# Logits' table on all partitions, T's copies ahead of V's last part, and four smaller moves in the front of a fused FFT, soft-MoE and ReLU² kernel

## The chip, the core and the metric

The kernel runs on one core of a Trainium2 chip. The metric is device time in microseconds: the median of several executions, before and after the change. The core has TensorE (matrix products into PSUM), VectorE, ScalarE and GpSimd for the rest, SyncE, whose queue issues nearly all transfers, and 16 DMA engines. In the rows PE is the matmuls of TensorE and PEld its weight loads; DVE is VectorE, ACT ScalarE, POOL GpSimd, SPq the queue of SyncE.

## The reference

The input x is 8 x 3072 x 256 in float32. Three layers follow one another:

```python
X = fft(fft(x, axis=1), axis=2).real                  # 24576 x 256
logits = X @ phi                                      # 8 experts x 4 slots
d = exp(logits - max over the 3072 positions); d /= d.sum(0) + 1e-9
c = exp(logits - max over the 32 slots);       c /= c.sum(1) + 1e-9
slots = d.T @ X;  slots = relu(slots @ w1[e]) @ w2[e] # per expert
Y = c @ slots                                         # 24576 x 256
out = (s * relu(Y @ w_in)**2 + b) @ w_out             # w_in 256 x 2048, w_out 2048 x 256, in float64
```

In the code the reshape to tokens runs over the batch and the positions of the FFT, and the maximum over a column is taken over all rows of the eight sequences together.

## The kernel before, in words

**Stages.** The FFT is never formed for logits: phi is folded into the DFT along the model dimension, and the DFT along the positions is split into 128 and 24. The front has five stages. (1) x comes in 24 pages of 1 MB, three for each of the eight sequences b. `emit_v(n)` (n = 2b and 2b + 1; the last is n = 15) multiplies pages by the folded phi (L394), copies the sum to `vts` (L406); `turn_v` transposes it (L415) and copies it to `v` (L419); `emit_t(b)` applies the DFT over 128 (L450, or L428 and L439 for the last b) and copies to `tt` (L464; L462 for b = 6; L432 and L445 for b = 7). (2) Logits: nine steps of products of `tt` with `ltab`, the table of the DFT over 24 (L570), for two halves of the partitions, h = 0 and 1; each sum is copied to `lg` (L583) and reduced to a column maximum (L585). The maxima are reduced again (L589, L592), transposed (L598), reduced (L603) and spread to all partitions as `cmb` (L608). (3) `lg - cmb` (L633, alternately VectorE and GpSimd), exp (L669), products with `htab`, the table of the second direction (L652). (4) The r stage: DFT of that and its sum with x's pages in another layout, `xrt` (24 pages of 1 MB, L326; products at L727). (5) The experts (w1, w2, 16 MB). Then the main loop over 64 blocks of 384 tokens, with the products at L1121, L1151 and L1154.

**Pages.** x, raw weights, tables and `xrt` share a ring of 15 pages of 8 KB per partition (20 from logits on). `page` takes one and `drop` gives it back; a transfer into a page waits for the last reader of the page's tile before. A string, `ORDER`, gives the order in which SyncE's queue gets its transfers in the front: x a page of x, w a quarter of w_out, r a page of `xrt`, l a page of `ltab`, h a page of `htab`. Eight transfers can be outstanding on that queue: the trace shows each issue behind the landing of the eighth before it.

**w_out** comes in float64 in four quarters, k = 0 to 3. A quarter is a list of side steps that the front hands out one at a time: five passes of VectorE that make float32 of it (s1 to s5), a maximum (L222), its sum into the bias on GpSimd (L276), its scale (L204, L205), the part rounded to f16 on ScalarE (`cast`, L212), and two steps `low`, the rest that rounding leaves (L216). For the last quarter, six steps (with two of the third quarter) stand before `emit_v(15)`, five in the rest of stage 1 and the two of `low` behind the logits.

**Around the change.** `emit_t(6)` holds its eight copies of T in a list, `late_t`: three go to ScalarE before the copy of V's last part, five behind it. Both pages of `ltab` come with 64 partitions of rows (two transfers each, of 32 partitions), and GpSimd copies them to the other 64:

```python
nc.gpsimd.tensor_copy(ltabs[0][0][64:P], ltabs[0][0][0:64])
nc.gpsimd.tensor_copy(ltabs[1][0][64:P], ltabs[1][0][0:64])
```

A page of `htab` has 48 rows in each half of the partitions; GpSimd clears rows 32 to 63 first (L350), and later the quarters that must be zero (`htab_clear`, L357), four operations behind the bias sums in its queue. `keep_warm(t, k)` issues k products of ones, which nothing reads.

## Time and profile before

| | us |
|---|---|
| median of 3 runs | 1401.25 (1399.19 to 1402.02) |
| the profiled execution, device time | 1403.16 |
| its span, first to last instruction | 1401.4 |
| TensorE busy, matmuls | 1377.4 (98%) |
| VectorE busy | 1163.4 (83%) |
| ScalarE busy | 1011.6 (72%) |
| GpSimd busy | 244.8 (17%) |
| mean granted TensorE clock | 0.997 of full speed |

The front ends with the first output product at about 228 us; the main loop takes the rest. A row of the stages gives busy time by engine, the granted clock (PEclk, 1.00 is 2.4 GHz) and the mean busy share and rate of the DMA engines. A row of the chain is a link of the chain of work that ended last, with its start and length. In a timeline row, the bracket gives the idle time of the engine before the group and what ended it; "issue" means that it waited for nothing that the profile shows.

### The profile page before, as it was taken

To read this page: it belongs to the slowest core of one execution; us is meant where nothing else is said; L and a number is where in the kernel's file an instruction comes from. 1 tells how busy PE (TensorE), PEld (TensorE's weight loads), DVE (VectorE), ACT (ScalarE), POOL (GpSimd) and SP (SyncE) were. 2 spreads that over 40 slices of the span, in tenths; PEclk is the share of its full clock that TensorE was granted. 3 is DMA by queue.
4 is the path that set the end of the run, shared out by engine and by line. 5 is a ranking of instruction groups with operands and counts; after the bars stand their busy time and mean duration, and the time that the engine had idled before them with its cause. 6 is when DMAs were issued, how large, how long until landed. Compare 5 with 4: busy or idle time off the path is not lost.

```text
span 1401.4 us, 23102 instructions
## 1 busy us (share of the span) xinstructions
PE 1377.4 (98%) x9036; PEld 843.8 (60%) x9036; DVE 1163.4 (83%) x1490; ACT 1011.6 (72%) x1423; POOL 244.8 (17%) x287
## 2 busy tenths in 40 slices
PE   9989999999999999999999999999999999999998
PEld 6667555566666666666666666666666666666665
DVE  1568745998989898989989898989888888888886
ACT  2666125777878787877777877777777777777775
POOL 1144200121212121212121111112111212111110
PEclk9999999999999999999999999999999999999999
DMA  8997992101010201010101101010101010101001
GB/s 348 414 311 304 365 410 104 36 24 36 20 33 23 37 22 34 23 37 23 36 24 27 32 20 35 21 37 24 32 24 37 23 37 24 37 24 36 18 21 31
DMA packets 72382, 112.27 MB, mean 80 GB/s; under 512 B 33905, under 2 KB 59633, under 8 KB 64977
## 3 DMA queue, kind: packets, MB, share of 16 engines
q1 hardware_dynamic: 72144, 110.70, 23.9%
q8 instruction: 71, 1.16, 0.3%
q14 instruction: 39, 0.31, 0.1%
q0 software_dynamic: 128, 0.10, 0.0%
HBM read 78.48 MB, written 25.17 MB: 74 GB/s over the span
## 4 chain that ended last, share of the span: by engine, by line
PE 89%; DMA 7%; DVE 2%; ACT 1%; issue 0%; POOL 0%; SPq 0%; DVEq 0%; ACTq 0%; POOLq 0%
PE op L1151 47%; PE op L1154 24%; PE fhp L1121 12%; DMA xb<-in_x_turned_dram 4%; PE racc L727 3%; DMA w2t<-in_moe_w_dram 2%; PE vt L394 1%; PE dps L712 1%; ACT dt L669 0%; PE lp L570 0%; ACT hh L643 0%; DVE cm L585 0%; DVE rhl L1112 0%; POOL dt L633 0%; DVE r L1127 0%
## 5 line engine op out<-in xcount | busy, mean ns | idle before, releaser
L1151 PE MATMUL op<-whl,rhl 128*128 128x512 f16 x3072 | 1025.2, 379 | 2.7 <-DVE ot L1164 1.7
L1154 PE MATMUL op<-whl,rhl 128*128 128x256 f16 x3072 | 835.7, 273 | 0.3 <-DVE rhl L1112 0.2
L1126 ACT ACTIVATE r<-fhp,wsc 128x768 f32<-128x768 f32 (+1 forms) x513 | 462.1, 901 | 229.8 <-PE fhp L1121 227.0
L1127 DVE SCALAR_TENSOR_TENSOR r<-fhp,r 128x768 f32<-128x768 f32 (+1 forms) x513 | 489.1, 954 | 123.4 <-ACT r L1126 112.9
L1151 PEld LDWEIGHTS <-rhl 128*128 128x128 f16 x3072 | 300.4, 98 | 335.9 <-ACT rhl L1111 1.1
L1112 DVE TENSOR_TENSOR rhl<-r,rhl 128x768 f16<-128x768 f32 x511 | 495.5, 970 | 2.3 <-ACT rhl L1111 2.2
L1111 ACT CAST rhl<-r 128x768 f16<-128x768 f32 x511 | 419.9, 822 | 3.5 <-DVE r L1127 3.5
L1154 PEld LDWEIGHTS <-rhl 128*128 128x128 f16 x3072 | 300.6, 98 | 65.4 <-issue 1.9
L1166 POOL TENSOR_TENSOR ot<-ot,bias 128x256 f32<-128x256 f32 x189 | 138.2, 732 | 962.9 <-DVE ot L1164 962.9
L1121 PE MATMUL fhp<-ct,g 128*128 128x384 f16 x1024 | 250.2, 326 | 0.7 <-POOL g L1086 0.7
L1121 PEld LDWEIGHTS <-g 128*128 128x128 f16 x1024 | 100.0, 98 | 68.0 <-POOL g L1086 1.2
L1163 ACT ACTIVATE o<-op,small 128x256 f32<-128x256 f32 x189 | 89.9, 476 | 16.1 <-PE op L1154 16.1
L1164 DVE SCALAR_TENSOR_TENSOR ot<-op,small,o 128x256 f32<-128x256 f32 x192 | 91.6, 478 | 0.3
L394 PE MATMUL vt<-xb,phd 128*64 128x384 f32 (+3 forms) x288 | 49.6, 482 | 6.0 <-DMA xb<-in_x_turned_dram 6.0
L727 PE MATMUL racc<-xrt,dh 128*64 128x256 f32 x384 | 44.5, 383 | 0.4 <-DVE dh L717 0.4
L394 PEld LDWEIGHTS vt<-xb,phd 128*64 128x64 f32 x288 | 26.1, 141 | 27.6 <-issue 10.1
L419 DVE COPY v<-vq 128x512 f32<-128x512 f32 (+1 forms) x15 | 8.3, 593 | 37.1 <-PE vq L415 37.1
L727 PEld LDWEIGHTS racc<-xrt,dh 128*64 128x64 f32 x384 | 26.3, 137 | 20.9 <-issue 4.9
L406 ACT COPY vts<-vt 128x512 f32<-128x512 f32 (+1 forms) x16 | 8.5, 533 | 38.7 <-PE vt L394 38.6
L464 ACT COPY tt<-tps 32x512 f32<-32x512 f32 x48 | 27.7, 577 | 5.3 <-PE tps L450 4.8
L756 POOL TENSOR_TENSOR lg<-et,lg 112x512 f16<-112x512 f32 x16 | 29.3, 1834 | 0.0
L774 POOL TENSOR_TENSOR lg<-lg,rm 112x512 f32<-112x512 f32 x16 | 22.4, 1404 | 3.9 <-DVE rm L772 3.9
(229 smaller groups left out, 509.4 us busy)
## 6 DMA issues: line engine op xcount, KB each, us to landing
xb<-in_x_turned_dram SPq DMA_DIRECT2D x24, 1024.0 KB, 20.1
xrt<-in_x_pages_dram SPq DMA_DIRECT2D x24, 1024.0 KB, 13.2
out_dram<-ot SPq DMA_DIRECT2D x128, 128.0 KB, 1.7
w1t<-in_moe_w_dram SPq DMA_DIRECT2D x8, 1024.0 KB, 13.6
out_dram<-ot SPq DMA_DIRECT2D x128, 64.0 KB, 2.0
raw<-in_moe_w_out_dram SPq DMA_DIRECT2D x4, 1024.0 KB, 20.9
raw<-in_moe_w_in_dram SPq DMA_DIRECT2D x4, 1024.0 KB, 8.2
w2t<-in_moe_w_dram SPq DMA_DIRECT2D x4, 1024.0 KB, 17.7
```

Source lines behind the costliest of these rows:

```text
L394: nc.tensor.matmul(vt[64 * h:64 * h + 64, o:o + k, :], lhsT=phd[:, c, sg, :], rhs=turned(pg, c, i, k, rev), start=(c == 0 and m < 2), stop ...
L727: nc.tensor.matmul(raccs[acc][64 * h:64 * h + 64, :], lhsT=dh[:, m, g].rearrange("p j e -> p (j e)"), rhs=xr[k][0][:, g, t, :], start=(sum ...
L1111: nc.scalar.copy(a, r2)
L1112: nc.vector.tensor_tensor(out=l, in0=r2, in1=a, op=ALU.subtract)
L1121: nc.tensor.matmul(hp[k * split][:, k, :].rearrange("p (s b m) -> p s b m", s=2, b=B), lhsT=g16[:, f * P:(f + 1) * P], rhs=c, start=True, ...
L1126: nc.scalar.activation(out=r[:, k], in_=hp[i][:, k], func=AF.Relu, scale=wsc[:, 2, p:p + 1])
L1127: nc.vector.scalar_tensor_tensor(out=r2[:, k], in0=hp[i][:, k], scalar=0.0, in1=r[:, k], op0=ALU.max, op1=ALU.mult)
L1151: nc.tensor.matmul(op.rearrange("p h d -> p (h d)"), lhsT=a, rhs=w.rearrange("p h d -> p (h d)"), start=(f == 0), stop=False)
L1154: nc.tensor.matmul(op[:, 0, :], lhsT=l, rhs=w[:, 0, :], start=False, stop=(f == NFC - 1))
L1163: nc.scalar.activation(out=o1, in_=op[:, 1, :], func=AF.Copy, scale=qv)
L1164: nc.vector.scalar_tensor_tensor(out=ot, in0=op[:, 0, :], scalar=qv, in1=o1, op0=ALU.mult, op1=ALU.add)
L1166: nc.gpsimd.tensor_tensor(out=ot, in0=ot, in1=bias, op=ALU.add)
```

## The change

Six edits. (1) `ltab`: four transfers of 32 partitions each, alternating between the two halves of the partitions and taking every second partition, fill one page, rows 0 to 31 of the table's second index in partitions 0 to 63 and rows 32 to 63 in 64 to 127; GpSimd copies both halves crosswise into the second page, and `ltab_of` picks the page. The tables go ahead of all pages of `xrt` in `ORDER`, the `htab` pages behind four of them; both `ltab` pages are dropped at the end of logits. (2) `htab`'s rows 48 to 63 are written by a transfer of zeros (16 rows that are zero in `ltab`) instead of a memset of rows 32 to 63. (3) All eight copies of `late_t` go ahead of V's last part; `turn_v(14)` too, with three warm-up products behind it; the copy to `vts` of n = 15 moves to VectorE; the side steps are dealt out anew, so that all of w_out is through before logits. (4) x's last page comes in two transfers, along the index c. (5) `low` of w_out's last quarter becomes two operations on GpSimd, in place. (6) The first ten pages of `xrt` come in two transfers of 4 KB per partition each. The early reduction of maxima takes eight groups instead of twelve, the last one nine instead of five.

```diff
@@ -213,8 +213,12 @@
...
         def low(j):
-            nc.vector.scalar_tensor_tensor(out=hl[:, 2 * j:2 * j + 2, 1, :], in0=w[:, 2 * j:2 * j + 2], scalar=inv[:, j:j + 1],
-                                           in1=hl[:, 2 * j:2 * j + 2, 0, :], op0=ALU.mult, op1=ALU.subtract)
+            l, f, h = hl[:, 2 * j:2 * j + 2, 1, :], w[:, 2 * j:2 * j + 2], hl[:, 2 * j:2 * j + 2, 0, :]
+            if k == 3:
+                nc.gpsimd.tensor_scalar(out=f, in0=f, scalar1=inv[:, j:j + 1], scalar2=None, op0=ALU.mult)
+                nc.gpsimd.tensor_tensor(out=l, in0=f, in1=h, op=ALU.subtract)
+            else:
+                nc.vector.scalar_tensor_tensor(out=l, in0=f, scalar=inv[:, j:j + 1], in1=h, op0=ALU.mult, op1=ALU.subtract)
             if j and k % 2:
@@ -286,7 +290,8 @@
...
         t, k = page([P, 2, 8, P], F32, "xb")
-        nc.sync.dma_start(out=t, in_=xt[3 * (n // 3) + (0, 2, 1)[n % 3]])
+        for c in (slice(0, 1), slice(1, 2)) if n == NX - 1 else (slice(0, 2),):
+            nc.sync.dma_start(out=t[:, c], in_=xt[3 * (n // 3) + (0, 2, 1)[n % 3]][:, c])
         xa.append((t, k))
@@ -294,7 +299,7 @@
...
     LEAD, TOL, LT, LX, HX = 14.0, 0.5, 0, 0, 1
-    ORDER = "xxxwxxxxxxwxxxxxxwxxxxwxrllhhrr"
+    ORDER = "xxxwxxxxxxwxxxxxxwxxxxwxllrrrrhh"
     tpool = tc.alloc_tile_pool(name="tpool", bufs=1)
@@ -323,7 +328,8 @@
...
         xr.append(page([P, NG, 2, D], F32, "xrt"))
-        nc.sync.dma_start(out=xr[i][0], in_=xp[i])
+        for g in (slice(0, 2), slice(2, 4)) if i < 10 else (slice(0, 4),):
+            nc.sync.dma_start(out=xr[i][0][:, g], in_=xp[i][:, g])
         dma_ready()
@@ -347,7 +353,8 @@
...
         htabs.append((t, k))
-        nc.gpsimd.memset(t[32:64], 0.0)
+        nc.sync.dma_start(out=t[M:64].rearrange("r k q m -> r (k q m)"),
+                          in_=ltab[M:64].rearrange("r q m -> r (q m)")[:, 0:128 * MH])
         for q in range(2):
@@ -359,10 +366,21 @@
...
         ltabs.append((t, k))
-        for c in range(2):
-            nc.sync.dma_start(out=t[NR * c:NR * c + NR], in_=ltab[64 * c:64 * c + M, 32 * i:32 * i + 32].rearrange(
-                "(j g) q m -> g j q m", j=2)[0:NR // 2])
-        dma_ready(2.57)
+        if i == 0:
+            l, w = ltab[0:1, 0:1, 0:1], P // 2
+            row = 64 * w
+            for j in range(2):
+                for h in range(2):
+                    nc.sync.dma_start(
+                        out=t[64 * h + j:64 * h + 64:2],
+                        in_=bass.AP(tensor=l.tensor, offset=l.offset + M // 2 * j * row + 32 * h * w,
+                                    ap=[[64 * row, 2], [row, NR // 2], [1, 32 * w]]),
+                    )
+            dma_ready(2.57)
+
+    def ltab_of(h, i):
+
+        return ltabs[(h + i) % 2][0][64 * h:64 * h + 64]
 
@@ -400,10 +418,7 @@
...
             vts[n] = xtp.tile([P, 4, P], F32, name="vts", bufs=2)
-            if n == 2 * B - 1:
-                for f in late_t[:3]:
-                    f()
-            nc.scalar.copy(vts[n][:, 0:ns], vt[:, 0:ns])
+            (nc.vector.tensor_copy if n == 2 * B - 1 else nc.scalar.copy)(vts[n][:, 0:ns], vt[:, 0:ns])
 
@@ -502,19 +517,22 @@
...
         emit_t(B - 2)
-        for _ in range(6):
+        for f in late_t:
+            f()
+        for _ in range(5):
+            side_step(0.0, True)
+        turn_v(2 * B - 2)
+        keep_warm(psv.tile([P, 4, P], F32, tag="vq", name="warm", bufs=2)[:, 0], 3)
+        for _ in range(2):
             side_step(0.0, True)
         emit_v(2 * B - 1)
-        for f in late_t[3:]:
-            f()
-        for n in range(2 * B - 2, 2 * B):
-            turn_v(n)
-        nc.gpsimd.tensor_copy(ltabs[0][0][64:P], ltabs[0][0][0:64])
-        nc.gpsimd.tensor_copy(ltabs[1][0][64:P], ltabs[1][0][0:64])
-        for _ in range(4):
-            side_step(0.0, True)
+        turn_v(2 * B - 1)
+        for h in (1, 0):
+            nc.gpsimd.tensor_copy(ltabs[1][0][64 * h:64 * h + 64], ltabs[0][0][64 - 64 * h:P - 64 * h])
+        side_step(0.0, True)
         emit_t(B - 1)
-        side_step(0.0, True)
+        while side_step(0.0, True):
+            pass
         load_xr()
@@ -568,13 +586,14 @@
...
                     nc.tensor.matmul(
-                        lps[h][q:q + m, k // 2, :], lhsT=ltabs[i8 // 4][0][r, 2 * KC * (i8 % 4) + k, 0:m],
+                        lps[h][q:q + m, k // 2, :], lhsT=ltab_of(h, i8 // 4)[:, 2 * KC * (i8 % 4) + k, 0:m],
                         rhs=tt[r, 2 * KC * i8 + k].rearrange("p b e -> p (b e)"), start=True, stop=True,
...
             for h, i8 in halves:
-                if h and i8 % 4 == 3:
-                    drop(ltabs[i8 // 4][1])
+                if h and i8 == NCH // 2 - 1:
+                    for _, k in ltabs:
+                        drop(k)
                 lp = lps[h]
@@ -585,11 +604,11 @@
...
                     nc.scalar.copy(dst, lp)
-                if done_l == NCH - 4:
-                    nc.vector.tensor_reduce(out=cm[:, NCH, :], in_=cm[:, :NCH - 4, :].rearrange("p i e -> p e i"), axis=AX.X,
+                if done_l == NCH - 8:
+                    nc.vector.tensor_reduce(out=cm[:, NCH, :], in_=cm[:, :NCH - 8, :].rearrange("p i e -> p e i"), axis=AX.X,
                                             op=ALU.max)
                 if done_l == NCH - 1:
-                    nc.vector.tensor_reduce(out=cm1, in_=cm[:, NCH - 4:, :].rearrange("p i e -> p e i"), axis=AX.X,
+                    nc.vector.tensor_reduce(out=cm1, in_=cm[:, NCH - 8:, :].rearrange("p i e -> p e i"), axis=AX.X,
                                             op=ALU.max)
@@ -597,8 +616,6 @@
...
         keep_warm(warm, 3)
-        while side_step(0.0, True):
-            pass
         cm2 = temps.tile([NE, 1], F32, name="cm2", bufs=1)
```

## Rows read from the trace of the kernel before

**Rows 1.** Page: busy us (share) x instructions; instruction queue: packets, MB, share.
```profile
PE 1377.4 (98%) x9036; PEld 843.8 (60%) x9036; DVE 1163.4 (83%) x1490; ACT 1011.6 (72%) x1423; POOL 244.8 (17%) x287
...
q8 instruction: 71, 1.16, 0.3%
```

**Rows 2.** Windows by stage of the front; the first line names the columns.
```profile
core 0: us, PE busy (x) PEld busy (x) DVE busy (x) ACT busy (x) POOL busy (x), PEclk, DMA share, GB/s
76.00:80.00 4.00, 4.00 (x28) 2.69 (x29) 2.58 (x5) 3.72 (x7) 2.94 (x3) 1.00 1.09 417
80.00:84.00 4.00, 3.22 (x22) 2.13 (x18) 3.75 (x4) 3.55 (x7) 0.00 (x0) 1.00 1.01 201
84.00:88.00 4.00, 2.73 (x14) 1.92 (x16) 0.00 (x0) 0.99 (x2) 0.00 (x0) 0.70 1.03 188
...
122.00:146.00 24.00, 22.90 (x203) 16.50 (x203) 19.55 (x38) 15.67 (x32) 16.51 (x16) 1.00 0.60 214
146.00:190.00 44.00, 44.00 (x358) 25.05 (x356) 33.55 (x43) 5.38 (x10) 2.53 (x3) 1.00 1.00 394
```

**Rows 3.** Chain of waits, 60 to 225: start us, us, what.
```profile
62.31 22.82 DMA xb<-in_x_turned_dram
...
100.56 1.58 issue
...
111.28 1.32 DVE whl L216 x2
...
191.51 18.59 DMA w2t<-in_moe_w_dram
```

**Rows 4.** Timeline, 76 to 98: start us, us, operation, count [idle before, releaser].
```profile
80.18 0.70 DVE L154 TENSOR_SCALAR wo<-raw 128x1024 uint32<-128x1024 uint32 x1 [0.41 <-DMA raw<-in_moe_w_out_dram]
...
85.27 4.06 PE L394 MATMUL vt<-xb,phd 128*64 128x384 f32 x20 [2.05 <-DMA xb<-in_x_turned_dram]
...
89.94 2.94 ACT L462 COPY tt<-tps 32x512 f32<-32x512 f32 x5
...
89.95 1.09 DVE L419 COPY v<-vq 128x512 f32<-128x512 f32 x2 [5.96 <-PE vq L415]
...
90.96 1.22 DVE L174 SCALAR_TENSOR_TENSOR wo<-raw,wo 128x1024 f32<-128x1024 uint32 x1
...
91.10 1.16 PE L428 MATMUL tpa<-f_sb,v 128*128 128x128 f32 x8 [0.58 <-DVE v L419]
...
92.06 1.89 POOL L512 COPY ltab<-ltab 64x2048 f32<-64x2048 f32 x1 [12.96 <-DMA ltab<-in_ltab_dram]
...
92.89 2.98 ACT L432 COPY tt<-tpa 32x256 f32<-32x256 f32 x8
...
95.92 2.34 PE L570 MATMUL lp<-tt,ltab 64*64 64x128 f32 x64 [1.52 <-ACT tt L432]
```

**Rows 5.** Timeline, 98 to 116, columns as above.
```profile
97.87 4.38 DVE L585 TENSOR_REDUCE cm<-lp 112x32 f32<-112x512 f32 x7 [2.27 <-ACT lg L583]
...
102.14 5.80 PE L570 MATMUL lp<-tt,ltab 64*48 64x128 f32 x128 [1.58 <-issue]
...
108.44 0.43 PE L570 MATMUL lp<-tt,ltab 64*64 64x128 f32 x4 [0.49 <-issue]
...
111.34 0.27 PE L598 MATMUL mt<-ident,cm 112*32 112x112 f32 x1 [0.72 <-DVE cm L592]
...
113.84 2.37 DVE L633 TENSOR_TENSOR dt<-lg,cmb 112x512 f32<-112x512 f32 x2
```

**Rows 6.** Lines: count, busy us, mean ns, idle us; GpSimd over the span.
```profile
L585 DVE TENSOR_REDUCE cm<-lp 112x32 f32<-112x512 f32 x16 | 10.1, 686 | 4.5 <-ACT lg L583 4.5
...
L756 POOL TENSOR_TENSOR lg<-et,lg 112x512 f16<-112x512 f32 x16 | 29.3, 1834 | 0.0
...
L276 POOL TENSOR_TENSOR bias<-bias,wo 128x256 f32<-128x256 f32 x14 | 10.2, 730 | 25.3 <-DVE wo L174 24.4
...
L357 POOL MEMSET htab_t<- 48x832 f32 x4 | 3.2, 788 | 0.2
```

## The prediction

> **What bounds the kernel now.** The page's busy times come first: TensorE is busy for 1377 of 1401 us [rows 1], nearly all of it in the main loop of output products, which no line of the diff touches. So only the front can change, and I read it by stages, then along the chain of waits, then instruction by instruction. The stages [rows 2] show a DMA queue that moves 417 GB/s up to 80 us, half of that (201 and 188 GB/s) from 80 to 88 us with its engines as busy as before, runs short of work from 122 to 146 us (share 0.60) and is full again from 146 to 190 us. The chain [rows 3] goes through x's last page (issued at 62.31, landed 22.82 later, at 85.13), the logits stage and its column maximum (the differences with it start at 113.84 [rows 5]), then TensorE's sums to 191.5 and the load of w2 behind them. So the front has two clocks. Until 114 us every step hands its time on. From 146 us the queue is full, but what fills it is pages that the r stage sets free, so an earlier r stage moves this end too. I therefore price the change at two places: the first product of logits (T0, now 95.92 [rows 4]) and the maximum (now 113.8).
>
> **T0 now.** Three things come late [rows 4]. The last raw part of w_out lands at about 80.15 (VectorE waited for it with the pass at 80.18). x's last page lands at 85.13; its 20 matmuls take 4.06, at a granted clock of 0.70 over that stretch [rows 2], so partly at the lower level, 1.2 GHz, after TensorE had been idle for 2.05, that is from 83.2. Then ScalarE copies V's part, five held-back parts of T (2.94) and eight of the last T (2.98), which T0 waits for. VectorE turns V at 89.95, twice, in 1.09.
>
> **T0 after.** All eight held-back copies of T stand ahead of V's last part: 0.59 each by the row of five, 4.7 from 83.2 on, so ScalarE is free at 87.9. VectorE does, from 80.18: three passes on the raw part (0.70, and 1.22 twice by the row of the like pass at 90.96) to 83.4; V's first turn (half of 1.09), once TensorE has transposed it, to 84.5; two more passes (0.7 and 1.22) to 86.4; the copy of V's last part, 0.5 by the turn's row, to 86.9; after 0.4 of transposes the second turn, to 87.9. x's last page must be summed by 86.4. At the full rate it would land 2.5 (1 MB at 417 GB/s) behind the raw part, at 82.65. It comes in halves along the loop over c, so only ten matmuls follow the second half: 1.0 to 2.0 by the row of 4.06. Even landing at 84.4 it costs nothing. From the turn on: T's products 1.16 and eight copies 2.98, with waits of 0.1, give T0 = 92.1, or 3.8 earlier.
>
> What speaks against all of the 3.8 is that logits' tables now stand one page nearer to x. The half rate began at about 80, with the tables queued behind x's last page and the first page of the sums; without that page between, it begins some 2.5 earlier and falls on the raw part too. If it costs as much as now, the raw part lands 2.5 later and T0 is 94.6, 1.3 earlier than now. If the four pieces, which alternate between partitions 0 to 63 and 64 to 127, share the load, it costs little. I take 1.0 of the 2.5: **T0 = 93.1, a gain of 2.8** (bounds 1.3 and 3.8). The table's two copies on GpSimd (1.89 each [rows 4]) start when the pieces have landed, 86 to 88, and end by 92, in time.
>
> The Trainium skill speaks against the first part of the change: "SBUF — State Buffer" (Door 1 and "Can I just issue two DMAs to hit both halves?") says that partitions 0 to 63 reach eight of sixteen ports, with an asymptote near 218 GB/s, and that two transfers to the two halves gained only 6% over one. The row of 201 GB/s agrees with the first statement; by the second the rate would stay halved, and T0 would be 94.6 rather than 93.1.
>
> **From T0 to the maximum**, 17.9 now. VectorE has sixteen reductions of 0.69, which start every 0.6 when nothing holds them (seven in 4.38 [rows 5]). It is idle for 4.5 before them [rows 6], 2.27 of it before the first [rows 5], so 2.2 between them. The cause is TensorE: at 100.56 it stops for 1.58 with no releaser ("issue" [rows 3]), and 128 matmuls, each with its weight load, later it stops again, for 0.49 [rows 5]. The instruction queue carried 71 packets for 2 x 9036 TensorE instructions [rows 1], one for some 255: the distance of the two stops. So these are waits for instructions, whose packets (1.16 MB in 71, 16 KB each) stand beside full data queues. After the change three added warm-up matmuls move this boundary some 12 instructions ahead, out of the last warm-up before T0, so the next block is asked for earlier; the data packets are 4 KB and, in that stretch, off the half rate. I count the 2.2 as gone; if the stops stay, it is 0.
>
> The last two passes of w_out's low part leave VectorE: they stand on the chain for 1.32 from 111.28 [rows 3]. Without them the next reduction starts behind the transpose (111.34 and 0.27 [rows 5]) at 111.7 instead of 112.6: 0.9. The longer last reduction (nine groups for five) gives back 0.2 and takes as much off the earlier one. Sum 2.2 + 0.9 - 0.2 = 2.9, bounds 0.7 and 2.9; I take 2.7, since the second boundary falls among the other tables' pieces. **The maximum is ready 5.5 earlier**, at 108.3 (bounds 2.0 and 6.7).
>
> **GpSimd** takes four instructions more. None in the trace has this form. Bounds for the four are 4 x 0.47 (a quarter of the 2048-element copy of 1.89) = 1.9 and 4 x 1.83 (the subtraction to f16 [rows 6]) = 7.3; I take 6.3, near the upper end, for the like subtraction. Its queue: table copies to 92, four bias sums of 0.73, the low part from 94.5 (ScalarE's rounded part is then there) to 101, clearing of the other tables (4 x 0.79 [rows 6]), a small cast, then logits' differences, for which it is due at 108.3. These tables now follow four 1 MB pages: 84 + 2.5 to 5 + 10 + 3.7 to 7.6, so they land at 100 to 107 and clearing ends at 104 to 108.3. Cover: 0 to 4. The zero rows come by DMA, which takes two memsets off GpSimd early, where it was idle. Dropping both table pages at the end of logits holds up no page that the queue could use before 105. Halving ten pages doubles their issues on SyncE; at 122 to 146 the DMAs have slack [rows 2], so nothing.
>
> **After the maximum** nothing is edited. The r stage starts 5.5 earlier and hands that to the w2 loads. The profiled execution took 1403.16, with a span of 1401.4; that is 1.9 above the median of 1401.25. 1403.16 - 5.5 = 1397.7; against the median, **1395.7**.
>
> **The rivals.** (a) The half rate stays: every piece goes to one half, all sixteen DMA engines meet there at once, and the raw part lands at 82.65. T0 gains 1.3, the rest 2.2 to 2.7: 1397.5. For it: 201 and 188 GB/s; against it: DMA engines drift apart, so that different pieces are in flight together. Chance 0.17. The page named above would have it so. (b) The instruction waits stay: 2.8 + 0.7 = 3.5, 1397.8. For it: the packet passes the same full queues; against it: the earlier boundary. Chance 0.15. (c) The gain is absorbed behind the r stage: the load behind the last sum took 18.59 to land [rows 3], so the queue's bytes could set the end whatever TensorE does; then 0 to 2 are left, 1400.3. Against it: the share of 0.60 at 122 to 146, ahead of the backlog. Chance 0.10. (d) GpSimd becomes the bound, and the kernel is slower: logits' differences wait in its queue behind the clearing of tables that now land behind four pages. It decides from 108.3 on, and outweighs the gain only if clearing ends after 113.8, with tables landing after 112, five later than my latest estimate. A second way into the same queue: the page of w_out, set free only by GpSimd's last low pass, may be handed to the last quarter of logits, which ScalarE then can't write. That GpSimd holds VectorE up can be seen: the first two differences took 2.37 with GpSimd's beside them, where a reduction of the same 112x512 takes 0.69 [rows 5, 6]. Price 1 to 4 beyond the gain: 1403.5. Chance 0.07.
>
> **How the numbers follow.** The forecast has 0.51, with its own range 1394.0 to 1397.2. A measurement of this kernel tells about 0.2% from no change, 2.8 us, so faster means below 1398.45. The forecast lies there, (a) and (b) mostly; (c) counts as the same, (d) as slower: faster 0.75, same 0.18, slower 0.07. The range reaches from the sum of the upper bounds (1394.5, and 1 of scatter) into (c): 1393.5 to 1400.0.
>
> **What would show it.** Right: T0 at 92 to 94, with no copies of T held back behind V's last part; no issue gap of over 1 in logits; no w_out pass on VectorE ahead of the maximum, this at 107 to 110; w2's end 5 to 6 earlier. Wrong: the raw part landing after 82; 200 GB/s for 8 us as before; a GpSimd difference that starts more than 0.3 behind the maximum; or an r stage earlier by 5 whose end is not. The forecast fails as a whole if the shift at the maximum does not arrive at the first output product.

## The result, and the profile after the change

The changed kernel is slower: 1416.93 us median (1415.29 to 1428.83, six runs) beside 1402.35 for the kernel before (1399.19 to 1404.76, six runs), a ratio of 1.0119 with a 95% interval of 1.0098 to 1.0139. That is some 15 us more, where 5.5 less was forecast. In single runs of some kernels the granted clock is lower and the time some 12 longer than in the others (one of the six above, at 0.981; four of e4's twelve, 1416 to 1418 at 0.987 to 0.988, without which its median is 1405.2). The profiled execution took 1417.94, with a span of 1416.1 us and a mean granted clock of 0.990 (before 0.997).

The chain of waits of the changed kernel, 60 to 250 us (start us, us, what), already names other links than [rows 3]:

```profile
65.22 20.59 DMA ltab<-in_ltab_dram
85.87 26.31 DMA xrt<-in_x_pages_dram
112.19 9.57 DMA htab_t<-in_htab_dram
...
123.70 0.28 POOL id L550
...
202.88 21.70 DMA w2t<-in_moe_w_dram
```

x's last page is gone from it. In its place stands the first piece of logits' table, then a page of the sums that SyncE could only issue once that piece had landed, then htab behind both, then GpSimd. The stages (columns as in [rows 2]) show what happened to the queue:

```profile
76.00:80.00 4.00, 4.00 (x23) 2.30 (x20) 3.58 (x6) 3.91 (x7) 0.00 (x0) 1.00 1.02 373
...
84.00:88.00 4.00, 2.75 (x69) 2.15 (x68) 2.17 (x3) 2.30 (x5) 0.00 (x0) 1.00 0.70 187
88.00:92.00 4.00, 1.48 (x36) 1.19 (x24) 1.71 (x4) 3.62 (x9) 0.00 (x0) 1.00 0.39 135
92.00:96.00 4.00, 0.00 (x0) 0.00 (x0) 0.00 (x0) 0.00 (x0) 0.00 (x0) 0.71 0.52 158
96.00:100.00 4.00, 2.40 (x26) 2.28 (x30) 0.00 (x0) 0.37 (x1) 1.89 (x1) 0.50 0.38 135
100.00:104.00 4.00, 4.00 (x84) 4.00 (x81) 1.98 (x3) 1.86 (x5) 0.50 (x1) 0.51 0.23 79
...
112.00:122.00 10.00, 3.85 (x22) 3.41 (x21) 5.44 (x11) 3.81 (x12) 3.87 (x5) 0.78 0.73 178
122.00:146.00 24.00, 22.40 (x203) 19.75 (x203) 16.37 (x31) 16.72 (x37) 15.90 (x15) 0.95 1.00 395
146.00:190.00 44.00, 43.76 (x350) 24.64 (x348) 34.17 (x48) 9.94 (x18) 10.83 (x11) 1.00 0.91 344
```

From 92 to 96 us no engine does anything, while the DMA engines are only half busy. So this is no full queue: few of the engines had work. The DMA view of 88 to 100 us, in 40 slices of 0.3 us, says how few:

```profile
GB/s 177 273 369 232 205 109 96 68 27 55 55 55 55 55 55 55 55 55 109 191 205 328 314 287 259 137 82 55 55 27 55 55 55 27 68 123 437 314 246 232
```

The rate sits at 55 GB/s for whole microseconds, and at 27 in single slices. Sixteen engines moved 417 GB/s [rows 2], 26 each; 55 is two engines. The trace also has the steps of the semaphore that counts a transfer's landing. For the first piece of the table there is one right behind the issue (66.3) and then only two, at 84.4 and 85.8; the first piece of e1, below, has sixteen, from 78.7 to 86.4.

The timeline, 76 to 126 us (columns as in [rows 4]):

```profile
82.00 2.38 PE L412 MATMUL vt<-xb,phd 128*64 128x384 f32 x20
...
87.37 2.99 ACT L447 COPY tt<-tpa 32x256 f32<-32x256 f32 x8 [1.67 <-PE tpa L443]
...
97.60 6.99 PE L588 MATMUL lp<-tt,ltab 64*64 64x128 f32 x112 [8.12 <-DMA ltab<-in_ltab_dram]
97.77 1.89 POOL L531 COPY ltab<-ltab 64x2048 f32<-64x2048 f32 x1 [22.47 <-DMA ltab<-in_ltab_dram]
...
103.50 1.89 POOL L531 COPY ltab<-ltab 64x2048 f32<-64x2048 f32 x1 [3.85 <-DMA ltab<-in_ltab_dram]
...
105.44 5.31 PE L588 MATMUL lp<-tt,ltab 64*64 64x128 f32 x144 [0.86 <-POOL ltab L531]
...
108.61 1.57 POOL L218 TENSOR_SCALAR wo<-wo,wsc 128x512 f32<-128x512 f32 x1
...
113.04 1.15 POOL L219 TENSOR_TENSOR whl<-wo,whl 128x512 f16<-128x512 f32 x1
114.23 2.05 ACT L602 COPY lg<-lp 112x512 f32<-112x512 f32 x4 [5.58 <-POOL whl L219]
...
119.89 0.79 POOL L364 MEMSET htab_t<- 48x832 f32 x1 [5.70 <-DMA htab_t<-in_htab_dram]
...
120.98 1.29 DVE L650 TENSOR_TENSOR dt<-lg,cmb 112x512 f32<-112x512 f32 x2
...
123.94 2.50 POOL L650 TENSOR_TENSOR dt<-lg,cmb 112x512 f32<-112x512 f32 x2
124.18 1.22 PE L669 MATMUL hp<-htab_t,dt 112*128 112x104 f32 x8 [0.21 <-POOL id L550]
```

Up to T everything came as forecast or earlier: x's last page is summed at 82.0 to 84.4, T's last copies end at 90.4. Then TensorE waits 8.1 for a piece of the table, GpSimd copies the table at 97.8 and 103.5 (forecast: done by 92), does its low part behind that at 108.6 to 114.2, and ScalarE waits 5.6 for it, since logits' last quarter stands in w_out's page. htab lands so late that GpSimd clears it until 123.6, and its first difference comes 3.0 behind VectorE's.

### The profile page after: what moved, and what is told of

Same layout as the page of the kernel before. It is cut to its first block, busy times and chain, and to the rows that moved or that the text cites. A ratio compares the mean times of both kernels' runs of the same rounds, so it can differ in the third digit from the quotient of the medians.

```text
span 1416.1 us, 23123 instructions
## 1 busy us (share of the span) xinstructions
PE 1380.4 (97%) x9042; PEld 845.2 (60%) x9042; DVE 1162.3 (82%) x1489; ACT 1010.9 (71%) x1422; POOL 246.6 (17%) x289
## 4 chain that ended last, share of the span: by engine, by line
PE 90%; DMA 8%; DVE 1%; ACT 1%; POOL 0%; issue 0%; SPq 0%; POOLq 0%; DVEq 0%; ACTq 0%
PE op L1168 46%; PE op L1171 24%; PE fhp L1138 12%; PE racc L744 3%; DMA xb<-in_x_turned_dram 2%; DMA xrt<-in_x_pages_dram 2%; PE vt L412 2%; DMA w2t<-in_moe_w_dram 2%; DMA ltab<-in_ltab_dram 1%; PE hp L669 1%; PE dps L729 1%; PE eop L974 1%; DMA htab_t<-in_htab_dram 1%; DVE r L1144 0%; PE tps L465 0%; DVE rhl L1129 0%
## 5 line engine op out<-in xcount | busy, mean ns | idle before, releaser
L1180 ACT ACTIVATE o<-op,small 128x256 f32<-128x256 f32 x189 | 89.9, 476 | 16.1 <-PE op L1171 16.1
L412 PEld LDWEIGHTS vt<-xb,phd 128*64 128x64 f32 x288 | 26.6, 139 | 25.1 <-issue 13.2
L604 DVE TENSOR_REDUCE cm<-lp 112x32 f32<-112x512 f32 x16 | 10.1, 686 | 17.1 <-ACT lg L602 17.1
## 6 DMA issues: line engine op xcount, KB each, us to landing
xb<-in_x_turned_dram SPq DMA_DIRECT2D x23, 1024.0 KB, 20.1
xrt<-in_x_pages_dram SPq DMA_DIRECT2D x20, 512.0 KB, 10.2
```

The lines of the kernel that those rows point to most:

```text
L412: nc.tensor.matmul(vt[64 * h:64 * h + 64, o:o + k, :], lhsT=phd[:, c, sg, :], rhs=turned(pg, c, i, k, rev), start=(c == 0 and m < 2), stop ...
L1180: nc.scalar.activation(out=o1, in_=op[:, 1, :], func=AF.Copy, scale=qv)
```

## The experiments

The time is best followed by stages. The first table gives, from each profiled execution's timeline: the start of VectorE's first pass on w_out's last raw part (L154); how far that pass lies behind the landing of the page of x ahead of the raw part in the queue; from the pass to the first product of logits; to the end of the last of these products; to the end of the copy that spreads the maximum; to the end of the last product with htab; from the end of the sums to the first output product. The sums between take 65.2 in every kernel and the main loop 1172.8 to 1173.2, so they stand in no column. All in us.

| kernel | raw pass at | behind x | to logits | logits | to maximum | to last htab product | sums' end to output |
|---|---|---|---|---|---|---|---|
| before | 80.2 | 2.8 | 15.7 | 13.0 | 4.9 | 16.3 | 33.0 |
| after | 77.9 | 2.7 | 19.7 | 13.2 | 10.2 | 18.7 | 38.5 |
| e1 | 79.3 | 3.5 | 13.2 | 13.0 | 4.5 | 17.9 | 36.1 |
| e2 | 79.6 | 3.7 | 11.8 | 14.6 | 5.1 | 16.3 | 34.8 |
| e3 | 77.4 | 2.7 | 20.4 | 20.1 | 5.4 | 17.8 | 33.2 |
| e4 | 81.1 | 4.8 | 13.4 | 16.1 | 4.2 | 16.2 | 37.1 |
| e5 | 82.2 | 5.4 | 12.6 | 14.8 | 4.6 | 16.3 | 33.0 |
| e6 | 78.6 | 3.2 | 12.5 | 12.7 | 4.6 | 16.3 | 35.7 |
| e7 | 80.9 | 4.1 | 12.2 | 12.0 | 4.6 | 16.3 | 33.4 |
| e8 | 77.8 | 2.7 | 12.5 | 14.4 | 3.9 | 16.3 | 33.7 |
| e9 | 79.1 | 3.3 | 13.4 | 9.8 | 4.8 | 17.8 | 35.1 |
| e10 | 81.0 | 4.1 | 12.7 | 12.9 | 3.9 | 16.3 | 32.9 |
| e11 | 82.4 | 5.7 | 17.1 | 10.5 | 4.2 | 16.2 | 33.7 |
| e12 | 80.8 | 3.7 | 11.6 | 13.8 | 3.6 | 16.3 | 33.2 |
| e13 | 81.2 | 4.6 | 12.9 | 11.4 | 4.8 | 16.2 | 35.2 |
| e14 | 79.1 | 3.3 | 12.2 | 14.5 | 4.0 | 16.2 | 33.3 |

The first column differs by 5 us between executions, and only a part of that is scatter upstream of every edit: the page of x ahead of the raw part lands at 74.6 to 77.4. The rest is the raw part itself. Where the table stands right behind x and its pieces have 16 outermost (e1, e2, e4 to e14), VectorE can start on the raw part 2.7 to 5.7 behind that page, 2.8 in the kernel before (the rate from 76 to 80 is 311 GB/s in e1 and 417 before [rows 2]). So a single profile must be read from that page on, and logits' start behind it is the sum of the second and the third column: 18.5 in the kernel before, 16.7 in e1. VectorE's wait for the raw part, and a later one for the sum of x's last page, in e5:

```profile
82.17 0.69 DVE L154 TENSOR_SCALAR wo<-raw 128x1024 uint32<-128x1024 uint32 x1 [3.02 <-DMA raw<-in_moe_w_out_dram]
...
88.82 0.56 DVE L418 COPY vts<-vt 128x384 f32<-128x384 f32 x1 [0.97 <-PE vt L409]
```

In the kernel before the first of these waits was 0.41 [rows 4].

The medians, against runs of the kernel before on the same chip:

| kernel | median (runs) | before | ratio, 95% interval |
|---|---|---|---|
| e1 | 1404.75 (11) | 1401.40 | 1.0025, 1.0011 to 1.0040 |
| e2 | 1406.81 (12) | 1401.40 | 1.0042, 1.0024 to 1.0060 |
| e3 | 1413.19 (4) | 1401.40 | 1.0108, 1.0068 to 1.0148 |
| e4 | 1407.54 (12) | 1401.40 | 1.0056, 1.0030 to 1.0082 |
| e5 | 1401.10 (12) | 1402.22 | 0.9999, 0.9980 to 1.0017 |
| e6 | 1401.55 (12) | 1402.22 | 0.9998, 0.9983 to 1.0012 |
| e7 | 1399.28 (12) | 1402.22 | 0.9984, 0.9969 to 0.9998 |
| e8 | 1398.62 (12) | 1402.22 | 0.9978, 0.9965 to 0.9991 |
| e9 | 1400.13 (12) | 1401.51 | 0.9983, 0.9958 to 1.0008 |
| e10 | 1400.35 (12) | 1401.51 | 0.9979, 0.9955 to 1.0004 |
| e11 | 1401.27 (12) | 1401.51 | 0.9992, 0.9965 to 1.0018 |
| e12 | 1399.57 (12) | 1401.51 | 0.9987, 0.9968 to 1.0006 |
| e13 | 1398.69 (12) | 1401.46 | 0.9977, 0.9957 to 0.9997 |
| e14 | 1398.95 (12) | 1401.46 | 0.9971, 0.9946 to 0.9996 |

### Two engines for a transfer (e1, e2, e3)

The theory (theory 1 below): a source whose outermost dimension is 2 puts a transfer on two DMA engines. The four pieces of the table all have it. The rivals: it is the stride of two partitions, or another edit altogether. e1 takes neighbouring partitions, 16 rows outermost:

```diff
-            for j in range(2):
+            for c in range(2):
                 for h in range(2):
                     nc.sync.dma_start(
-                        out=t[64 * h + j:64 * h + 64:2],
-                        in_=bass.AP(..., ap=[[64 * row, 2], [row, NR // 2], [1, 32 * w]]),
+                        out=t[64 * h + NR * c:64 * h + NR * c + NR],
+                        in_=ltab[64 * c:64 * c + M, 32 * h:32 * h + 32].rearrange("(j g) q m -> g j q m", j=2)[0:NR // 2],
```

> The changed kernel, with logits' page again filled by four transfers of 256 KB, but each of 32 neighbouring partitions (one c, one h), so that the source runs over 16 rows in its outermost dimension, where the change has 2. Theory 1 (a transfer whose outermost dimension is 2 runs on two of the sixteen DMA engines, and that alone costs the time): the four pieces land within 3 us of each other before 90, the first product of logits is at 91 to 93, the first difference at 107 to 110, and the time is 1395 to 1399. Rival 2 (taking every second partition makes the transfer slow): the same, since the stride is gone too. Rival 3 (the loss lies in another edit: the order of the pages, the low part on GpSimd, the halved pages): the time stays within 4 of the changed kernel's 1417.

e2 keeps the stride and cuts each piece in two along c, so that its source begins with 16 rows:

```diff
-                        out=t[64 * h + j:64 * h + 64:2],
-                        in_=bass.AP(..., ap=[[64 * row, 2], [row, NR // 2], [1, 32 * w]]),
+                        out=t[64 * h + NR * c + j:64 * h + NR * c + NR:2],
+                        in_=bass.AP(..., ap=[[row, NR // 2], [1, 32 * w]]),
```

> The changed kernel, with its every-second-partition form kept, but each of its four transfers cut in two over c: eight transfers of 128 KB whose outermost source dimension is 16 rows. Theory 1 (two engines because of the outermost 2): fast, within 2 of the kernel with 32 neighbouring partitions, 1395 to 1400. Rival 2 (the stride of two partitions): the pieces still land 3 us or more apart, the last after 98, and the time stays above 1410.

e3 puts the form of the change, and nothing else, into the kernel before:

```diff
-        for c in range(2):
-            nc.sync.dma_start(out=t[NR * c:NR * c + NR], in_=ltab[...].rearrange("(j g) q m -> g j q m", j=2)[0:NR // 2])
+        for j in range(2):
+            nc.sync.dma_start(out=t[j:64:2], in_=bass.AP(..., ap=[[64 * row, 2], [row, NR // 2], [1, 32 * w]]))
```

> The kernel before, with one edit alone: each of logits' two pages is filled by two transfers of 256 KB that take every second partition, with 2 as the outermost dimension of the source, as the change has it (two transfers per page, as before). Theory 1: the four transfers run one after another on two DMA engines, 5 to 6 us each, the last lands at 100 to 106, the first product of logits moves from 95.9 to 98 to 102, and the time is 1408 to 1420. Rival 3 (the loss lies in another edit): within 3 of the kernel before.

In e1 the table lands by 89.6, in e2 by 86.1, and logits begin 13.2 and 11.8 behind the raw part. The stride of two partitions costs nothing that can be seen there; the outermost 2 was the cause (e2's median is 2.1 above e1's, with intervals that overlap). e3 shows that this form is enough by itself: 11.8 us on the kernel before. Its timeline, 90 to 120 us:

```profile
97.70 6.19 PE L572 MATMUL lp<-tt,ltab 64*64 64x128 f32 x112 [9.88 <-DMA ltab<-in_ltab_dram]
...
110.08 7.69 PE L572 MATMUL lp<-tt,ltab 64*64 64x128 f32 x144 [6.20 <-DMA ltab<-in_ltab_dram]
```

TensorE waits for the table twice, 9.9 and 6.2. The second wait ended at 110, later than the 100 to 106 that I expected of the last piece. The Trainium skill has the rule ("DMA: Bandwidth & Descriptors", section "Why a DMA increments its semaphore by 16 and not by 1"): a transfer gets the largest number of engines up to 16 that divides the slowest dimension of both its sides. The 55 GB/s agree with it.

But e1 is not at 1395 to 1399, nor e2 at 1395 to 1400. With the table mended the change still loses 0.25%, so theory 1 held for its mechanism and not for "that alone". The table of stages says where: counted from the page of x, logits begin 1.8 earlier than before, they take as long as before, and two later stages, with 1.6 and 3.1 more, give back more than was gained. The timeline of e1, 76 to 126 us (L585 are logits' products, L364 clears htab, L647 the differences, L666 the products with htab):

```profile
92.50 3.05 PE L585 MATMUL lp<-tt,ltab 64*64 64x128 f32 x82 [0.93 <-ACT tt L444]
...
99.40 6.06 PE L585 MATMUL lp<-tt,ltab 64*48 64x128 f32 x137 [2.01 <-issue]
...
106.99 0.78 POOL L364 MEMSET htab_t<- 48x832 f32 x1 [5.43 <-DMA htab_t<-in_htab_dram]
...
109.98 1.29 DVE L647 TENSOR_TENSOR dt<-lg,cmb 112x512 f32<-112x512 f32 x2
...
112.17 2.95 POOL L647 TENSOR_TENSOR dt<-lg,cmb 112x512 f32<-112x512 f32 x2
...
114.15 12.04 PE L666 MATMUL hp<-htab_t,dt 112*128 112x104 f32 x105 [1.36 <-ACT dt L683]
```

Logits have a stop of 2.0 without a releaser, like the 1.58 of the kernel before [rows 3]. GpSimd's first difference comes 2.2 behind VectorE's, because it was clearing htab until 111.9. The 3.1 lie between the sums and the output.

### Pages handed on (e5), htab first (e6), both (e7), whole pages (e8)

What e1 loses behind the sums shows in SyncE's waits, 140 to 165 us (line, waited for: us in total, times, longest), of e1:

```profile
SPq L150 <- PE racc L741: 7.3, 2, 4.6
SPq L150 <- DVE wi L174: 5.5, 1, 5.5
```

L150 loads the raw parts of w_in. One of them waits for VectorE, where in the kernel before all four waited for the sums. The cause lies in the order in which pages are taken and given back. The change brings all of w_out through before logits, so its last page is given back earlier, and five pages of the sums, not four, find a place in the first ring. From then on the loads behind them get other slots: the first raw part that of the sixth page of the sums instead of the fifth, the third the slot of the first raw part itself, which is free only behind VectorE's passes. e5 puts the give-back where it was:

```diff
-            if j and k % 2:
-                drop(wok[k // 2])
+            if j and k == 1:
+                drop(wok[0])
...
-        load_xr()
         keep_warm(psv...)
...
         keep_warm(warm, 3)
+        drop(wok[1])
```

> The changed kernel with logits' page on sixteen rows (as in the first of these runs), and w_out's last page given back at the end of logits, as in the kernel before, with one page of the sums fewer ahead of logits: so the ring of pages hands the same slots to the first two loads of w_in as before. With the table mended, TensorE's sums ended 2.3 earlier than before (193.0 for 195.3), yet the last w2 transfer landed 0.9 later (221.3 for 220.5): the first load of w_in waited for the sixth group of sums (issued at 148.6) where before it waited for the fifth, and the third for VectorE's passes on the first (160.2, before 157.4). Theory P (those two page handovers swallow the gain): the first load of w_in is issued at 145 to 146, the third at 155 to 156, the last w2 transfer lands at 217.5 to 219.5, the median is 2 to 4 below the mended kernel's 1404.75. Rival Q (the bytes of the full DMA queue set the end, whatever page is used): the two loads are issued earlier, but the last w2 transfer still lands at 220 to 222 and the median is within 1 of 1404.75.

The same view of e5:

```profile
SPq L150 <- PE racc L741: 8.1, 4, 4.4
```

All four loads wait for the sums again. This execution's front was 2.9 later than e1's from the first column on, so the absolute times I expected don't hold (issues at 147.9 and 157.8), but the distance from the sums' end to the output is back at 33.0, and the median fell by 3.65 (on another chip; by the ratios it is 3.6, and their intervals overlap a little). Theory P held, Q not. Every kernel with the pages of the change has 34.8 to 38.5 in that column, every one with the old pages and an undisturbed queue 32.9 to 33.7.

e6 changes the order of the queue in e1, e7 does both, e8 takes whole pages besides:

```diff
-    ORDER = "xxxwxxxxxxwxxxxxxwxxxxwxllrrrrhh"
+    ORDER = "xxxwxxxxxxwxxxxxxwxxxxwxllhhrrrr"
```

> The changed kernel with logits' page on sixteen rows, and htab's two pages ahead of the four pages of the sums instead of behind them. There GpSimd cleared htab's rows until 111.9, as its transfers landed at 107 to 111, and its first difference of logits began at 112.2, 2.2 behind VectorE's, so that the products with htab stopped for 1.4. Theory G (GpSimd's clearing holds the differences): the clearing ends before 107, GpSimd's first difference is within 0.2 of VectorE's, the products with htab and all sums come 1.2 to 2.2 earlier; the median is 1 to 2 lower if the w_in loads pass it on. Rival (the tables queue beside logits and take the DMA rate from something that TensorE needs): the maximum itself is later by 1 or more, and the median is not lower.

> The two edits of this call together: the pages handed out as before, and htab ahead of the sums' pages. If theories P and G both hold their gains add: the first output product comes 3.5 to 5.5 earlier than in the mended kernel, the median is 1399 to 1401.5, a little under the kernel before. If Q holds: within 1.5 of 1404.75.

```diff
-        for g in (slice(0, 2), slice(2, 4)) if i < 10 else (slice(0, 4),):
-            nc.sync.dma_start(out=xr[i][0][:, g], in_=xp[i][:, g])
+        nc.sync.dma_start(out=xr[i][0], in_=xp[i])
```

> The kernel with both edits of this call, and the first ten pages of the sums in whole transfers of 8 KB per partition, as before. It prices the halving by itself. If the 4 KB packets shorten TensorE's waits for instructions in logits: the stop that lasted 2.0 in the mended kernel is longer, and the median is 0.5 to 2 above the same kernel with halves. If the size of the packets does nothing: within 0.7 of it.

With htab first GpSimd starts 0.1 behind VectorE, the stage to the last htab product is 16.3 as before, and the median falls by 3.2, a little more than the 1 to 2 expected; 1.6 of it is GpSimd's. The two add up in the main: e7 at 1399.28 is 5.5 below e1, where 3.65 and 3.2 would make 6.9, and 0.16% under the kernel before. e8, 0.22% under it, is the same as e7 within the interval: the 4 KB packets do nothing that can be measured.

### The stops in logits (e9, e13, e14)

Logits' products take 9.8 to 16.1 (20.1 in e3, which waits for the table), mostly by how long TensorE stops without a releaser. The theory: it waits for its own instructions, whose packets pass full data queues. e9 leaves the queue empty in the second half of logits: the list `gate[0]` has the pages held back, VectorE writes one column into the first of them behind the seventh step, and SyncE waits for it.

```diff
+            if st == 6:
+                nc.vector.memset(xr[0][0][:, 0, 0, 0:1], 0.0)
+                for i in gate[0]:
+                    nc.sync.dma_start(out=xr[i][0], in_=xp[i])
+                gate[0] = None
```

> The kernel with both mends, htab ahead and whole pages of the sums (the last of the call before, 1398.6), with the first ten pages of the sums held back: VectorE writes one column of the first of them behind the reductions of logits' seventh step, and SyncE's queue waits for that, so that few data packets move while TensorE is in the second half of logits. Theory B (TensorE's stops without a releaser are waits for instruction packets behind full data queues): the stops in logits, 2.1 and more in that kernel, shrink to under 0.6 each once tables have landed, logits take 10.3 to 11.5 from the first product to the last where they took 12.0 to 14.8 in the kernels so far, and the median is 1 to 3 lower if the sums' pages still come in time. Rival (the stops have nothing to do with the data queues): they stay at 1.4 to 2.1, and the median is the same or higher.

Logits in e8, then in e9 (timeline, 88 to 112 us):

```profile
90.31 3.05 PE L583 MATMUL lp<-tt,ltab 64*64 64x128 f32 x82 [0.93 <-ACT tt L443]
93.60 1.62 PE L583 MATMUL lp<-tt,ltab 64*64 64x128 f32 x37 [0.24 <-DVE cm L599]
97.35 7.32 PE L583 MATMUL lp<-tt,ltab 64*48 64x128 f32 x137 [2.12 <-issue]
```

```profile
92.51 9.78 PE L587 MATMUL lp<-tt,ltab 64*64 64x128 f32 x256 [0.93 <-ACT tt L447]
```

Not one stop is left, and 256 products take 9.8; the instruction packets come sooner, too (last section). So, as far as one profile can show it, the full queue is what the stops need, though it doesn't bring them every time: e11, below, lost 0.3 in all beside a full queue. The stages of e9 show what it was paid with (columns as in [rows 2]):

```profile
96.00:100.00 4.00, 3.74 (x109) 2.77 (x101) 4.00 (x8) 3.71 (x8) 3.84 (x5) 1.00 0.01 4
...
108.00:112.00 4.00, 3.79 (x27) 3.55 (x26) 1.95 (x3) 2.49 (x6) 2.61 (x2) 0.73 1.01 428
...
122.00:146.00 24.00, 22.90 (x194) 14.31 (x194) 18.73 (x37) 11.73 (x23) 15.57 (x15) 1.00 1.01 419
```

The queue, nearly still from 92 to 104, is full from 108 on, through the stretch in which it had slack before (0.60 in [rows 2]). Of the 4.6 that e9's logits take less than e8's nothing is left at the output: logits begin 0.9 later behind the raw part and the maximum comes 0.9 later behind logits, the stage to the last htab product takes 1.5 more, with a granted clock of 0.73 from 108 to 112, and the time behind the sums 1.4 more, 35.1. The median is not lower than e8's. e13 and e14 let the first three pages go ahead of the gate, e14 with e2's eight pieces for the table:

```diff
-        if gate[0] is None:
+        if gate[0] is None or i < 3:
...
-                nc.vector.memset(xr[0][0][:, 0, 0, 0:1], 0.0)
+                nc.vector.memset(xr[3][0][:, 0, 0, 0:1], 0.0)
```

> The kernel that holds the sums' pages back (1400.1), but with the first three pages let go at once; the gate stands on the fourth. In that kernel logits lost no time to stops (9.8 for 12.0 to 14.8), yet the queue of w2 landed no earlier, since it was full from 108 us to the end. Theory Q' (what is taken from the queue during logits has to be paid back behind the sums): with three pages, 7.5 us of transfers, moved ahead, the time from the end of the sums to the first output product falls from 35.1 to 33 to 34, and the median to 1397 to 1399. Rival (the first pages fill the queue while TensorE waits for its instructions): stops of over 0.5 come back, logits take over 11, and the median is 1399 to 1401.

> The same with the eight pieces of every second partition, sixteen rows each, for logits' table. The profile of that form showed x's last page 1 earlier than with four pieces, twice, and the first product of logits 1 earlier. If this comes through: 0.5 to 1 lower than with four pieces. If not: within 0.7.

The stops came back, 1.5 in e13 and 3.9 in e14: the three pages fill the queue just when the instructions are due (a DMA share of 1.02 from 96 to 100 in both), and when it has run empty there is no second stop. The time behind the sums was 35.2 in one and 33.3 in the other, with the same pages held back and the queue as full from 112 to 190, so theory Q' (33 to 34) held in e14 and not in e13, and it is not shown that held pages cost anything there, in e9 either. Both medians, 1398.7 and 1399.0, are those of e8.

### Single terms of the sum (e4, e10, e11, e12)

e4 undoes the table's form within the change (both pages into partitions 0 to 63 alone, copied up), e11 does so in e8:

```diff
+        for c in range(2):
+            nc.sync.dma_start(out=t[NR * c:NR * c + NR], in_=ltab[64 * c:64 * c + M, 32 * i:32 * i + 32]...)
...
-            nc.gpsimd.tensor_copy(ltabs[1][0][64 * h:64 * h + 64], ltabs[0][0][64 - 64 * h:P - 64 * h])
+            nc.gpsimd.tensor_copy(ltabs[i][0][64:P], ltabs[i][0][0:64])
```

> The changed kernel without its first edit's form: both of logits' pages come as in the kernel before, 64 partitions of rows each, copied by GpSimd to the other 64, while their place in the order and all other edits stay. The bytes are the same as in the four pieces of 32 partitions. If loads into partitions 0 to 63 alone run at half the rate: x's last page lands 2 to 4 later than with the pieces that alternate between the halves, the first product of logits is at 94 to 96, and the time is 1 to 3 above that kernel. If the halves don't matter: within 1 of it.

> The same kernel (1398.6) with both of logits' pages loaded as before, into partitions 0 to 63 alone, and copied up by GpSimd. If it matters that the pieces go to both halves of the partitions (the forecast's reason for an undisturbed load of x's last page): x's last page lands 1.5 or more later behind the raw part of w_out than the 4.6 of that kernel, the first product of logits comes 1 to 2 later behind it than 12.5, and the median is 1 to 2 higher. If the halves don't matter: 4.2 to 5.6, 12.2 to 13.2, and the median within 1.

Behind the raw part x's last page lands 6.0 later in e4, 5.8 in e1; 6.5 in e11, 4.5 to 5.3 in e5 to e8. At 417 GB/s [rows 2] it would be 2.5, and it is 2.6 in the changed kernel, where the table took two engines and left the others to x. So the half rate stayed whichever half the pieces went to. The raw part is late as well, so the page of x ahead of it is the better start: behind that, x's last page lands 10.8 later in e4 and 9.3 in e1, 12.1 in e11 and 7.3 in e8; but e5 to e8, with the same pieces, spread from 7.3 to 10.6. By the Trainium skill ("SBUF — State Buffer", "Can I just issue two DMAs to hit both halves?") two transfers to the two halves reached only 6% more than one; that spread is too wide for these runs to show it or to speak against it. e11's logits begin 17.1 behind the raw part, since TensorE, idle while it waited for x, was granted 0.50 of its clock (the lower level, 1.2 GHz) from 92 to 96. e11's median is 2.6 above e8's, where 1 to 2 was expected if the halves matter, and e4's is 2.8 above e1's, where it was 1 to 3, but the intervals of the ratios overlap in both pairs. Both point to a gain by the form; the runs don't settle its size.

e10 has the low part of w_out's last quarter on VectorE again, behind the last reduction:

```diff
-            if k == 3:
-                nc.gpsimd.tensor_scalar(out=f, in0=f, scalar1=inv[:, j:j + 1], scalar2=None, op0=ALU.mult)
-                nc.gpsimd.tensor_tensor(out=l, in0=f, in1=h, op=ALU.subtract)
-            else:
-                nc.vector.scalar_tensor_tensor(...)
+            nc.vector.scalar_tensor_tensor(...)
```

> The same kernel (1398.6) with the low part of w_out's last quarter back on VectorE behind the last reduction, as before. It prices that edit by itself: by my sum the maximum moves back by 0.7 to 0.9, from 3.9 to 4.6 behind the last product of logits to about 4.8, and the median is 0.5 to 1 higher. If GpSimd's four operations had cost as much as they gave (GpSimd late for the differences): no change.

From the end of the last reduction of maxima to the spread maximum it takes 2.52 in e10 and 1.64 in e8: 0.88, for the 0.9 of the sum. In the stage (3.9 in both, where 4.8 was expected) and the median (0.9979 for 0.9978) it is not to be seen.

e12 has e2's eight pieces in e8.

> The same kernel (1398.6) with the eight pieces of every second partition, sixteen rows each, in place of the four pieces. In the earlier pair of runs x's last page landed 3.7 behind the raw part with the eight pieces and 5.9 with the four, and the first product of logits came 11.8 and 13.2 behind it. If that was the form of the pieces: 1 to 1.5 earlier here too, and a median 0.5 to 1.5 lower. If it was the scatter from one execution to the next: the same within 0.7.

x's last page comes 3.5 behind the raw part and logits 11.6, as in e2. But the raw part itself is 1.0 later than in e8, and behind the page ahead of that, x's last page comes 7.2 later in e12 and 7.3 in e8. In the other pairs the eight pieces are earlier (7.4 in e2 and 9.3 in e1, 8.0 in e14 and 10.1 in e13). So a gain of this form is not shown, and the median has none.

## Why the prediction was wrong

**The step that failed first** is the one on the table's pieces: GpSimd's copies "start when the pieces have landed, 86 to 88, and end by 92, in time". I costed the pieces by their bytes at the queue's rate, full or half, and never asked how many engines each would use; each ran on two engines, 5.5 to 6.2, one behind the other (the first landed at 85.8, the others were there at 92, 97.5 and 103.4). e1 against the changed kernel prices it: medians 12 apart, 13 by the ratios of 1.0025 and 1.0119. No rival of mine had it; (a), the half rate, was the nearest, with a price of 1.8.

**T0**, once this is taken away, came near the forecast, but only on average and partly by luck. Counted from the page of x ahead of the raw part, it is 0.5 to 3.3 earlier in e1 and e5 to e8 than in the kernel before, 2.1 on average, where I took 2.8. The half rate did stay, as (a) said, and it did fall on the raw part, which landed up to 2.6 later behind that page, 1.0 on average: what I had charged for it. The path behind it was another. I had VectorE's passes as the last link, and x's last page as free if it landed by 84.4. VectorE was through with the passes and waited 0.4 to 1.5 for that page's sum, since its second half landed 4.6 to 5.8 behind the raw part, where I had allowed 4.2.

**Logits** were wrong. I counted 2.2 of VectorE's idle time as gone, since the boundary of the instruction blocks would move and the packets be smaller. The stops were there in nearly every kernel that kept the queue full, 1.4 to 5.6 together (e11 alone lost 0.3), and logits took as long in e1 as before. Rival (b) held (0.15), and e9 shows its condition, full data queues. The packets' size made no difference that shows: 1.4 to 5.6 with halved pages, 0.3 to 3.3 with whole ones beside a full queue.

**The low part** was right in both its sizes: 0.9 off VectorE's path (e10: 0.88), and 5.4 on GpSimd for my 6.3. What I had as its cover was wrong. **Rival (d)** (0.07) came true in both its ways, with the slow pieces ahead of them. In the changed kernel GpSimd's clearing ended at 123.6, and w_out's page was logits' last quarter and held ScalarE for 5.6. With the pieces mended the clearing still ended at 111.9 (e1), 3.6 behind the latest that I had allowed, because htab's transfers, behind four pages and at a low rate (190 GB/s from 96 to 104), landed at 107 to 111 and not at 100 to 107; price 1.6.

**After the maximum** I wrote that nothing was edited and that the r stage would hand its gain to the loads. The sums did, 65.2 in each kernel. The loads did not: by giving w_out's last page back earlier the change had moved every later page to another slot, and a load of w_in came to wait for VectorE. That cost 3.1 in the profiles and some 3.6 in the medians (e5 against e1), more than logits' earlier start had gained. It is a term that my sum lacked; I had asked only whether a page would be held up "before 105". Rival (c), the queue's bytes, was not the reason: with the old pages (e5, e7, e8) the stage is back at 33.0 to 33.7. Whether the bytes are the bound where e9 holds pages back stays open, since e13 and e14 differ there by 1.9.

**The sum again**, from the page of x ahead of the raw part, e7 against before: 2.2 in front of logits (3.5 behind the raw part, which itself came 1.3 later), 1.0 in them (two stops, then one), 0.3 to the maximum, 0 behind it, 0.4 lost at the end: 3.2 in the profiles, 2.9 in the medians, where 5.5 was forecast for the change as it stood.

## What to carry to other kernels

Where a transfer's pattern is rewritten, read the outermost dimension of its source and destination before its bytes: 256 KB took 5.5 to 6.2 us by two engines, and pieces with 16 outermost gave 12 to 13 us back. A transfer moved nearer in the queue can also delay what stands ahead of it (up to 2.6 us here): count from a landing that no edit can move, or the cost drops out of the comparison. Where pages or buffers are handed on in turn, an earlier give-back moves every later one to another slot, so follow the map of who waits for whom to the end of the program, not to the end of the edited stage. And a gain in a stretch with a full data queue lasts only if TensorE's own instructions come through it too.

## What the runs showed of the hardware

TensorE's instructions came further apart beside full data queues. They come in packets of 16 KB, one for some 255 instructions by the prediction's count. In the kernel before they started 6.2 and 6.0 us apart in and behind logits (99.8, 106.0, 112.0); with the queue nearly empty in e9 they came 4.1 and 4.0 apart (93.1, 97.2, 101.2), and TensorE did not stop. The packets themselves took about as long, 1.0 to 1.1 and 0.9 to 1.1.

A stop costs more than itself where the granted clock falls behind it. In e8, after 2.1 of waiting, the clock was 0.55 from 96 to 100 and 0.59 from 100 to 104, and 137 products took 7.3; in e13, after 1.5, it stayed at 1.00 and the same 137 took 5.1. The stages of e8, then of e13:

```profile
96.00:100.00 4.00, 2.65 (x52) 2.65 (x56) 1.56 (x3) 1.04 (x2) 3.92 (x4) 0.55 0.98 406
100.00:104.00 4.00, 4.00 (x86) 4.00 (x80) 3.58 (x7) 2.41 (x6) 2.76 (x5) 0.59 1.02 420
```

```profile
96.00:100.00 4.00, 2.68 (x72) 1.95 (x65) 3.48 (x6) 3.48 (x7) 3.84 (x4) 1.00 1.02 403
100.00:104.00 4.00, 3.51 (x115) 3.27 (x118) 2.81 (x6) 2.64 (x6) 3.86 (x5) 1.00 0.37 152
```

The time at which the same loads have landed differs by 2.8 us from one execution to another (74.6 to 77.4 for the page of x ahead of the raw part), while the main loop, 1173 us long, agrees within 0.4.
